# K^T V products as four 64x64 tiles, K rectified in place, and routing split into single steps, in a fused attention and adapter kernel

## The chip, the cores and the metric

The kernel runs on one core of a Trainium2 chip. A core has TensorE for matrix products (PE in the profile; its weight loads stand apart as PEld), VectorE (DVE), ScalarE (ACT), GpSimd (POOL, which here issues the loads from memory) and SyncE (SP, which issues the stores). The metric is the time of one execution on the device, in microseconds, as the median of several runs. The profile is of one execution and counts from its first instruction to its last; that span is a little shorter than the time.

## The reference

Two parts, one after the other. First a linear attention over 8 batches, 8 heads, 576 positions and 64 values per head; q and k are rectified and weighted with a cosine and a sine of the position. Then a layer that picks 2 of 8 small adapters for each of the 4608 rows and adds their output.

```python
def phi(x, c, s):
    r = np.maximum(x, 0.0)
    return np.concatenate([r * c, r * s], axis=-1)
q_p = phi(q, cos_w, sin_w)
k_p = phi(k, cos_w, sin_w)
kv = np.einsum('bhsf,bhsd->bhfd', k_p, v)
z = np.sum(k_p, axis=2)
num = np.einsum('bhsf,bhfd->bhsd', q_p, kv)
den = np.einsum('bhsf,bhf->bhs', q_p, z)[..., None] + 1e-06
x = num / den                       # then laid out as 4608 x 512
# ... (cut: the layer that picks adapters)
logits = x @ w_gate                 # 8 logits a row, the best 2 are kept
# w = softmax over the kept two
delta = sum over kept e of w[e] * ((x @ A[e]) @ B[e])
out = x + delta
```

The cosine and the sine are put on V instead of K, so that K needs the rectifier alone: each V row becomes `V*cos, cos` and `V*sin, sin` (2 x 65 columns), and K^T times that gives kv and z at once.

## The kernel before

Every piece of work is a step of a plan: an engine, an emitter, what it needs and which buffers it uses. Three tables, found ahead of time and written into the file, fix everything that a scheduler would choose: ORDER is the order of all steps (and so of the instructions on each engine, which run in that order), CHOICE takes one of the engines that a step may run on, and SLOTS gives each use its buffer. HOLD lists (store, load): the store waits until that load has landed.

The loads cast from 32 to 16 bits on their way. For a batch b: K is rectified into a second buffer KR whose order is position block, head, value; V is scaled twice into VV; two steps `kv`, one for each pair of heads a, multiply; and each of these is copied out of PSUM by two steps `kvev` into BD, a block-diagonal operand for the products with q.

```python
POOLS = {"V": 4, "K": 3, "KR": 3, "Q": 5, "VV": 3, "BD": 4, ..., "OSB": 6, ..., "pND": 2, "pS": 4}

def relu_k(eng, hs, uk, ukr):                       # K -> KR
    i = tK[S_(uk)][:, hs[0]:hs[-1] + 1]
    o = tKR[S_(ukr)].rearrange("p j c d -> p c j d")[:, hs[0]:hs[-1] + 1]
    # ACT: activation Relu;  DVE: max with 0

def kv_mm(a, ukr, uvv, up):                         # 18 matmuls, 64 rows x 128 columns, 260 wide
    for j in range(J):                              # J = 9
        for par in range(2):
            r = slice(64 * par, 64 * par + 64)
            nc.tensor.matmul(
                out=pt[:, par, 0:4 * W], lhsT=kt[r, j, 2 * a:2 * a + 2, :],   # W = 65; two heads side by side
                rhs=vt[r, 2 * a:2 * a + 2, j, :][:, :, :, 0:W],               # (views shortened here)
                start=(j == 0), stop=(j == J - 1), skip_group_check=True)

def kv_evac(a, hh, up, ubd, eng):                   # 64 x 260, one head
    o = tBD[S_(ubd)][r, :, a, :, 66 * hh:66 * hh + W]
    i = pND[S_(up)][r, :, hh * 2 * W:(hh + 1) * 2 * W]
```

A matmul there multiplies two heads with two heads (128 x 260), and half of that product, head times the other head's V, is never read.

The rest works on 36 groups of 128 rows. A group goes through: transposes of q (`qt`), rectifier while copied out (`qtev`, ACT), times the tangent (`tan`, DVE), products with BD (`num`), reciprocal of den (`rden`, DVE), `xt` = num times that (DVE), transposes (`xT`), copy (`xTev`), logits and A products of up to three groups (`za`), routing, `zgT`, and the sum with B products (`dx`), copied out (`osb`) and stored. The last nine groups take half of their rows from batch 6 and half from batch 7, so they need kv of both. The routing of three groups:

```python
def r_max(uza, n, um):
    for i in range(n):
        nc.vector.max(out=m8[:, i], in_=lg[:, i])                 # best logits of each row
    nc.vector.tensor_reduce(out=tNA..., in_=m8[:, 0:n, 0:2], ...)  # minus the sum of the two best
    nc.vector.scalar_tensor_tensor(out=tTT..., in0=lg, scalar=2.0, in1=tNA..., ...)
def r_zg(uza, n, uw, uzg):
    nc.vector.tensor_tensor(out=w, in0=mask_v(uza, n), in1=tSG..., op=ALU.mult)
    nc.vector.tensor_tensor(out=tZG..., in0=za_v(...), in1=w..., op=ALU.mult)
# between the two: a sigmoid on ACT, and a mask on DVE
```

`r_max` is one step of the plan and so is `r_zg`: their instructions stand directly behind each other, and each reads what the one ahead of it wrote.

Of the kernel before, what the change touches and what calls it, by code (L numbers as in the profile page):

```python
# [11 lines left out]
BF16 = mybir.dt.bfloat16  # L12
# [8 lines left out]
    17, 32, 14, 15, 1, 19, 27, 16, 20, 0, 34, 2, 18, 26, 9, 11, 13, 23, 10, 45, 35, 3, 4, 33, 31, 30, 22, 12, 28, 7,  # L21
    24, 21, 29, 50, 8, 46, 5, 48, 49, 44, 51, 37, 52, 36, 38, 6, 62, 25, 41, 39, 40, 63, 142, 43, 134, 143, 150, 42,
    64, 158, 135, 144, 151, 145, 136, 159, 53, 86, 137, 146, 152, 160, 138, 139, 75, 147, 153, 140, 154, 148, 155, 47,
    76, 161, 149, 156, 141, 157, 162, 56, 163, 74, 55, 164, 57, 422, 58, 165, 87, 54, 182, 174, 423, 183, 166, 59,
    167, 425, 184, 175, 168, 190, 60, 61, 198, 191, 176, 169, 88, 65, 192, 177, 170, 171, 178, 179, 193, 172, 194,
    199, 185, 173, 180, 67, 98, 181, 424, 437, 66, 186, 187, 214, 99, 230, 200, 215, 71, 426, 231, 216, 427, 232, 188,
    72, 206, 195, 428, 189, 433, 438, 100, 207, 201, 89, 434, 429, 439, 440, 202, 73, 431, 208, 430, 203, 68, 432,
    441, 196, 79, 110, 70, 442, 204, 69, 222, 443, 209, 205, 78, 444, 223, 448, 445, 217, 210, 449, 224, 446, 111,
    218, 211, 197, 262, 254, 263, 451, 219, 454, 255, 264, 212, 447, 220, 256, 225, 455, 221, 453, 238, 213, 226, 112,
    227, 270, 233, 239, 77, 435, 228, 456, 271, 246, 457, 240, 83, 247, 458, 229, 248, 470, 85, 272, 84, 234, 235,  # L30
    459, 80, 450, 460, 471, 123, 91, 472, 236, 81, 463, 82, 465, 237, 473, 241, 474, 464, 461, 466, 242, 243, 475,
    249, 462, 469, 90, 244, 476, 257, 468, 245, 122, 477, 250, 251, 286, 479, 478, 258, 259, 481, 287, 278, 480, 265,
    452, 279, 482, 252, 260, 253, 92, 266, 280, 261, 288, 267, 485, 124, 93, 101, 94, 268, 273, 486, 269, 95, 488,
    274, 487, 275, 489, 276, 96, 294, 302, 97, 277, 490, 295, 289, 102, 491, 281, 303, 492, 290, 296, 496, 282, 493,
    103, 494, 497, 502, 495, 318, 283, 326, 319, 310, 291, 104, 311, 320, 327, 503, 107, 106, 328, 105, 304, 504, 113,
    334, 109, 284, 292, 108, 505, 305, 506, 285, 297, 293, 306, 312, 507, 335, 342, 298, 299, 508, 343, 114, 300, 313,
    115, 513, 301, 511, 307, 518, 314, 315, 321, 519, 509, 329, 322, 323, 514, 336, 119, 344, 510, 330, 331, 520, 512,
    308, 521, 316, 522, 121, 337, 515, 120, 317, 126, 523, 345, 524, 324, 309, 332, 338, 339, 525, 325, 529, 333, 346,
    347, 527, 526, 125, 533, 484, 530, 127, 528, 116, 531, 340, 534, 532, 118, 348, 128, 117, 536, 349, 535, 341, 537,
    131, 130, 129, 538, 350, 133, 374, 539, 351, 358, 132, 540, 359, 352, 544, 375, 360, 398, 353, 541, 545, 399, 361,  # L40
    376, 546, 354, 355, 366, 382, 362, 367, 542, 363, 390, 383, 400, 356, 377, 391, 500, 368, 384, 543, 369, 498, 378,
    392, 357, 406, 370, 414, 371, 407, 364, 550, 436, 379, 365, 415, 385, 408, 551, 372, 393, 553, 373, 386, 387, 483,
    380, 552, 566, 554, 381, 409, 394, 499, 395, 555, 388, 501, 567, 556, 396, 401, 517, 569, 397, 410, 416, 548, 559,
    568, 402, 389, 570, 557, 516, 560, 580, 403, 467, 558, 571, 411, 547, 561, 572, 404, 581, 564, 575, 405, 549, 583,
    562, 417, 582, 576, 563, 584, 412, 577, 413, 565, 573, 418, 419, 578, 585, 594, 574, 586, 420, 595, 587, 579, 421,
    589, 597, 596, 588, 591, 598, 610, 590, 592, 599, 611, 600, 605, 593, 601, 613, 612, 602, 606, 614, 617, 604, 603,
    615, 607, 608, 616, 618, 609, 620, 619, 621,
]
CHOICE = [
    0, 0, 0, 0, 0, 0, 0, 0, 0, 0, 0, 0, 0, 0, 0, 0, 0, 0, 0, 0, 0, 0, 0, 0, 0, 0, 0, 0, 0, 0, 0, 1, 0, 0, 0, 1, 0, 0,  # L50
    0, 1, 0, 0, 1, 1, 0, 0, 0, 1, 0, 1, 0, 0, 0, 0, 0, 0, 0, 0, 1, 0, 1, 0, 0, 0, 0, 1, 0, 0, 0, 0, 0, 0, 0, 0, 0, 0,
    0, 0, 0, 0, 0, 0, 0, 0, 0, 0, 0, 0, 0, 0, 0, 0, 0, 0, 0, 0, 0, 0, 0, 0, 0, 0, 0, 0, 0, 0, 0, 0, 0, 0, 0, 0, 0, 0,
    0, 1, 0, 0, 0, 0, 0, 0, 0, 0, 0, 0, 0, 0, 0, 1, 0, 0, 1, 1, 0, 0, 0, 0, 0, 0, 0, 1, 0, 0, 0, 0, 0, 0, 0, 1, 0, 0,
# [3 lines left out]
    0, 0, 0, 0, 0, 0, 0, 0, 0, 0, 0, 1, 0, 0, 0, 0, 0, 0, 0, 0, 0, 0, 0, 0, 0, 0, 0, 0, 0, 0, 0, 0, 0, 0, 0, 1, 0, 0,  # L57
    0, 0, 0, 0, 0, 0, 0, 0, 0, 0, 0, 0, 0, 0, 0, 0, 0, 0, 0, 0, 0, 0, 0, 0, 0, 0, 0, 0, 0, 0, 0, 0, 0, 0, 0, 0, 0, 1,
    0, 0, 0, 0, 0, 0, 0, 1, 0, 0, 0, 0, 0, 0, 0, 0, 0, 0, 0, 0, 0, 0, 0, 0, 0, 0, 0, 0, 0, 0, 0, 0, 0, 0, 0, 0, 0, 0,
    0, 0, 0, 0, 0, 0, 0, 0, 0, 0, 0, 0, 0, 0, 0, 0, 0, 0, 0, 0, 0, 0, 0, 0, 0, 0, 0, 0, 0, 0, 0, 0, 0, 0, 0, 0, 0, 0,  # L60
    0, 0, 0, 0, 0, 0, 0, 0, 0, 0, 0, 0, 0, 0, 0, 0, 0, 0, 0, 0, 0, 0, 0, 0, 0, 0, 0, 0, 0, 0, 0, 0, 0, 0, 0, 0, 0, 0,
    0, 0, 0, 0, 0, 0, 0, 0, 0, 0, 0, 0, 0, 0, 0, 0, 0, 0, 0, 0, 0, 0, 0, 0, 1, 0, 1, 0, 0, 0, 0, 0, 0, 0, 0, 0, 0, 0,
    0, 0, 0, 0, 0, 0, 0, 0, 0, 0, 0, 0, 0, 0, 0, 0, 0, 0, 0, 0, 0, 0, 0, 0, 0, 0, 0, 0, 0, 0, 0, 0, 0, 0, 0, 0, 0, 0,
    0, 0, 0, 0, 0, 0, 0, 1, 0, 1, 0, 0, 0, 0, 0, 0, 0, 0, 0, 0, 0, 0, 0, 0, 0, 0, 0, 0, 0, 0, 1, 0, 0, 0, 0, 0, 0, 0,
    0, 0, 0, 0, 0, 0, 0, 0, 0, 0, 0, 0, 0, 0, 0, 0, 1, 0, 0, 0, 1, 0, 0, 0, 0, 0, 0, 0, 0, 0, 0, 0, 0, 1, 1, 0, 0, 0,
    0, 0, 0, 0, 0, 0, 0, 0, 0, 0, 0, 0, 0, 0,
]
SLOTS = [
    3, 1, 0, 2, 0, 0, 0, 0, 0, 0, 0, 1, 1, 1, 1, 1, 1, 1, 1, 0, 2, 2, 2, 2, 2, 0, 2, 0, 1, 3, 3, 1, 0, 1, 3, 1, 0, 0,
    4, 0, 1, 0, 0, 0, 2, 1, 0, 2, 2, 0, 1, 1, 0, 2, 1, 1, 0, 1, 2, 0, 1, 3, 2, 0, 1, 0, 3, 1, 1, 1, 1, 1, 0, 0, 0, 0,  # L70
    0, 0, 0, 1, 1, 1, 2, 2, 1, 2, 2, 2, 2, 3, 3, 0, 1, 3, 3, 3, 3, 6, 1, 0, 4, 2, 4, 2, 5, 0, 2, 5, 0, 5, 0, 4, 0, 0,
    6, 1, 0, 0, 7, 1, 1, 7, 2, 1, 3, 0, 1, 2, 8, 0, 2, 0, 3, 1, 0, 9, 1, 3, 2, 1, 0, 1, 10, 0, 4, 3, 6, 1, 2, 11, 1,
    5, 0, 2, 0, 0, 12, 2, 0, 3, 4, 0, 1, 13, 0, 1, 3, 3, 1, 2, 14, 2, 2, 0, 7, 0, 0, 15, 1, 3, 1, 5, 1, 1, 2, 0, 4, 0,
    0, 1, 2, 0, 2, 5, 3, 6, 0, 1, 1, 3, 0, 2, 1, 1, 0, 3, 1, 1, 1, 2, 1, 1, 5, 1, 2, 0, 4, 0, 2, 4, 2, 3, 3, 5, 1, 0,
    7, 1, 4, 2, 3, 0, 1, 8, 0, 5, 1, 7, 1, 2, 6, 1, 0, 2, 0, 1, 0, 9, 3, 1, 0, 1, 0, 1, 10, 2, 2, 2, 6, 0, 2, 11, 3,
    3, 1, 2, 1, 0, 12, 0, 4, 3, 3, 1, 2, 14, 2, 5, 3, 4, 0, 1, 13, 0, 0, 2, 7, 1, 0, 0, 0, 1, 1, 0, 0, 2, 2, 3, 2, 1,
    5, 0, 0, 15, 3, 3, 2, 1, 1, 1, 1, 3, 4, 1, 6, 0, 2, 5, 2, 5, 1, 0, 0, 0, 2, 0, 1, 0, 0, 2, 3, 1, 1, 1, 1, 1, 1, 1,
    3, 0, 2, 0, 0, 0, 3, 0, 2, 2, 1, 3, 0, 1, 1, 1, 1, 1, 3, 3, 1, 0, 3, 0, 0, 0, 3, 0, 2, 4, 3, 1, 0, 1, 1, 1, 3, 1,
    1, 5, 3, 2, 0, 0, 0, 0, 3, 0, 3, 1, 0, 2, 1, 1, 1, 1, 0, 1, 0, 1, 0, 2, 3, 0, 0, 0, 2, 0, 3, 0, 2, 2, 1, 1, 1, 1,
    1, 1, 1, 3, 1, 2, 0, 0, 0, 0, 0, 0, 0, 4, 1, 2, 3, 1, 1, 1, 3, 1, 2, 5, 1, 0, 0, 0, 0, 0, 0, 3, 2,  # L80
# [3 lines left out]
    (435, 74), (451, 76), (452, 88), (484, 122), (500, 124),  # L84
# [65 lines left out]
def kernel(  # L150
# [10 lines left out]
    nc = tc.nc  # L161
# [20 lines left out]
    def sb(shape, dtype, name, n=None):  # L182
        if n is None:
# [4 lines left out]
    POOLS = {"V": 4, "K": 3, "KR": 3, "Q": 5, "VV": 3, "BD": 4, "QT": 8, "XT": 16, "XTT": 6,  # L188
             "ZG": 2, "ZGT": 2, "OSB": 6, "M8": 2, "W": 2, "RD": 3,
# [24 lines left out]
    tKR = sb([128, J, 4, D], BF16, "KR", POOLS["KR"])  # L214
# [16 lines left out]
    def S_(u):  # L231
        return pl.slot[u]
# [125 lines left out]
    pl.add("w", [("DVE", 0.6, w_aw("DVE")), ("ACT", 0.8, w_aw("ACT"))], 3, needs=["Ald", "Gld"], makes=["AW"])  # L358
# [25 lines left out]
    def relu_k(eng, hs, uk, ukr):  # L384
        def f():
            i = tK[S_(uk)][:, hs[0]:hs[-1] + 1]
            o = tKR[S_(ukr)].rearrange("p j c d -> p c j d")[:, hs[0]:hs[-1] + 1]
            if eng == "ACT":
                nc.scalar.activation(o, i, AF.Relu)
            else:  # L390
                nc.vector.tensor_scalar(out=o, in0=i, scalar1=0.0, scalar2=None, op0=ALU.max)
        return f

    def vscale(eng, cs, hs, uv, uvv):
        def f():
# [6 lines left out]
            else:  # L402
                nc.vector.tensor_tensor(out=o, in0=i, in1=TV[:, cs].unsqueeze(1).to_broadcast([128, n, J, D]), op=ALU.mult)  # L403
        return f

    def kv_mm(a, ukr, uvv, up):
        def f():
            kt, vt, pt = tKR[S_(ukr)], tVV[S_(uvv)], pND[S_(up)]
            for j in range(J):
# [328 lines left out]
```

## Time and profile before

The time is 117.64 us, the median of 3 runs (116.33 to 118.29). The profiled execution has a span of 115.4 us.

| Engine | busy us | share of the span | instructions |
|---|---|---|---|
| PE, matmuls | 96.9 | 84% | 1383 |
| PEld, weight loads | 68.8 | 60% | 1394 |
| DVE | 95.6 | 83% | 273 |
| ACT | 83.0 | 72% | 182 |
| POOL | 25.7 | 22% | 41 |

The page also has the span cut into 40 equal slices of 2.9 us, in which a digit is a tenth of busy time, and the chain of work that ended last, followed back from the end. Matmuls overlap in the array, so the busy time of PE is not what it could do at best; it is read together with when the matmuls start. In the lines of groups, the two numbers behind the first bar are the busy time of the group in us and the mean duration of one instruction in ns, and behind the second bar stands the idle time of the engine just ahead of them.

### The profile page before, as it was taken

What the parts mean: (1) busy time and instruction counts of PE and PEld (TensorE: products, weight loads), DVE (VectorE), ACT (ScalarE), POOL (GpSimd) and SP (SyncE); (2) the same over time, 40 slices, a digit from 0 to 9 for tenths busy, and PEclk for the clock granted to TensorE, in tenths of its full rate; (3) what the DMA queues carried; (4) which work ended last, traced back from release to release, by engine and by line L of the source; (5) the groups of instructions that cost most, each with busy time, mean ns of one, the idle gap of its engine ahead of it and who ended that gap; (6) DMA issues with size and microseconds to landing.
All of it is one profiled execution on the core that took longest, in us unless ns stands there. A gap on an engine that the chain in (4) does not pass through costs nothing.

```text
span 115.4 us, 3462 instructions
## 1 busy us (share of the span) xinstructions
PE 96.9 (84%) x1383; PEld 68.8 (60%) x1394; DVE 95.6 (83%) x273; ACT 83.0 (72%) x182; POOL 25.7 (22%) x41
## 2 busy tenths in 40 slices
PE   0999957679669999999999998979999999998600
PEld 0344445567556577876587787757676788665100
DVE  6823479979799999999999999999998999998700
ACT  5639477266947899979676889997846975989400
POOL 5997766352022222222200000000000000000000
PEclk9999999999999999999999999999999999999995
DMA  0999999999999999999999999999384298989991
GB/s 3 146 134 193 192 204 206 207 208 207 209 206 208 207 209 206 227 302 242 213 303 230 208 208 207 211 204 256 115 185 87 54 226 264 288 247 240 419 411 51
DMA packets 17039, 24.08 MB, mean 209 GB/s; under 512 B 2176, under 2 KB 14592, under 8 KB 17024
## 3 DMA queue, kind: packets, MB, share of 16 engines
q0 software_dynamic: 14096, 14.43, 75.7%
q1 hardware_dynamic: 2928, 9.44, 26.1%
q8 instruction: 11, 0.18, 0.6%
q14 instruction: 4, 0.03, 0.1%
HBM read 28.85 MB, written 9.44 MB: 332 GB/s over the span
## 4 chain that ended last, share of the span: by engine, by line
PE 43%; DVE 21%; DMA 14%; ACT 9%; issue 5%; POOL 3%; POOLq 0%; ACTq 0%; DVEq 0%
DMA Kb<-in_k_dram 14%; PE pnd L506 10%; PE pnd L412 10%; PE ps L530 5%; PE ps L476 5%; PE ps L602 4%; DVE xt L522 4%; DVE VV L403 4%; PE ps L543 4%; DVE qTcs L493 3%; PE ps L604 3%; ACT qTcs L481 3%; PE ps L591 2%; DVE zg L582 2%; ACT osb L242 2%
## 5 line engine op out<-in xcount | busy, mean ns | idle before, releaser
L522 DVE TENSOR_TENSOR xt<-pnd,rden 128x512 bf16<-128x512 f32 x36 | 24.3, 687 | 0.8
L506 PE MATMUL pnd<-BD,qTcs 128*128 128x130 bf16 (+1 forms) x384 | 22.5, 223 | 2.9 <-DVE xt L522 2.4
L481 ACT ACTIVATE qTcs<-ps 128x512 bf16<-128x512 bf16 x36 | 20.3, 602 | 5.5 <-PE ps L476 5.3
L403 DVE TENSOR_TENSOR VV<-Vb,TV 128x2304 bf16<-128x2304 bf16 (+1 forms) x17 | 19.1, 1135 | 4.0 <-DMA Vb<-in_v_dram 4.0
L506 PEld LDWEIGHTS <-qTcs 128*128 128x128 bf16 (+1 forms) x384 | 18.0, 103 | 6.2 <-issue 3.7
L412 PE MATMUL pnd<-VV,KR 64*128 64x260 bf16 x288 | 19.3, 272 | 2.7 <-DVE VV L403 1.2
L242 ACT COPY xT<-ps 128x512 bf16<-128x512 bf16 x30 | 17.1, 587 | 2.3 <-PE ps L530 1.9
L242 ACT COPY osb<-ps 128x512 f32<-128x512 f32 (+1 forms) x31 | 16.4, 574 | 1.9 <-DVE osb L244 0.9
L412 PEld LDWEIGHTS <-KR 64*128 64x128 bf16 x288 | 13.3, 93 | 6.8 <-issue 2.5
L493 DVE TENSOR_TENSOR qTcs<-qTcs,TT 128x512 bf16<-128x512 bf16 x36 | 14.0, 409 | 1.3 <-ACT qTcs L481 0.7
L530 PE MATMUL ps<-ident,xt 128*128 128x128 bf16 x144 | 13.3, 223 | 0.7 <-DVE xt L522 0.6
L602 PE MATMUL ps<-xt,ident 128*128 128x512 bf16 x35 | 13.1, 380 | 0.7 <-DVE osb L244 0.3
L424 ACT CAST BD<-pnd 64x260 bf16<-64x260 f32 x24 | 9.0, 376 | 5.6 <-PE pnd L412 4.5
L476 PE MATMUL ps<-ident,Qb 128*64 128x128 bf16 x288 | 11.9, 222 | 1.0 <-DMA Qb<-in_q_dram 0.7
L297 PE MATMUL ps<-warm 128*128 128x512 bf16 x34 | 9.2, 435 | 3.1 <-DVE warm L291 3.1
L401 ACT ACTIVATE VV<-Vb,TVf 128x128 bf16<-128x128 bf16 (+1 forms) x27 | 9.2, 433 | 3.5 <-DMA Vb<-in_v_dram 3.5
L530 PEld LDWEIGHTS <-xt 128*128 128x128 bf16 x144 | 9.5, 116 | 3.6 <-DVE xt L522 1.5
L476 PEld LDWEIGHTS <-Qb 128*64 128x64 bf16 x288 | 8.8, 109 | 4.5 <-issue 2.8
L543 PE MATMUL ps<-AW,xT 128*128 128x136 bf16 x144 | 10.8, 223 | 0.3 <-ACT xT L242 0.2
L543 PEld LDWEIGHTS <-xT 128*128 128x128 bf16 x144 | 9.1, 98 | 2.3 <-issue 0.8
L604 PE MATMUL ps<-Ball,zgT 128*128 128x512 bf16 x26 | 9.7, 379 | 0.4 <-ACT zgT L242 0.4
L297 PEld LDWEIGHTS <-warm 128*128 128x128 bf16 x34 | 3.6, 109 | 7.9 <-DVE warm L291 3.1
(54 smaller groups left out, 107.2 us busy)
## 6 DMA issues: line engine op xcount, KB each, us to landing
out_dram<-osb SPq DMA_DIRECT2D x16, 256.0 KB, 4.5
Kb<-in_k_dram POOLq DMA_DIRECT2D x6, 576.0 KB, 22.8
Vb<-in_v_dram POOLq DMA_DIRECT2D x6, 576.0 KB, 24.8
Qb<-in_q_dram POOLq DMA_DIRECT2D x6, 576.0 KB, 24.8
out_dram<-osb SPq DMA_DIRECT2D x6, 384.0 KB, 4.5
out_dram<-osb SPq DMA_DIRECT2D x2, 768.0 KB, 5.7
Kb<-in_k_dram POOLq DMA_DIRECT2D x4, 288.0 KB, 7.4
Vb<-in_v_dram POOLq DMA_DIRECT2D x4, 288.0 KB, 6.9
```

What stands on the lines that cost most here:

```text
L242: nc.scalar.copy(o, i)
L403: nc.vector.tensor_tensor(out=o, in0=i, in1=TV[:, cs].unsqueeze(1).to_broadcast([128, n, J, D]), op=ALU.mult)
L412: nc.tensor.matmul(out=pt[:, par, 0:4 * W], lhsT=kt[r, j, 2 * a:2 * a + 2, :].rearrange("p h d -> p (h d)"), rhs=vt[r, 2 * a:2 * a + 2, j, ...
L476: nc.tensor.transpose(out=pt[64 * hh:64 * hh + 64, a, :, x], in_=qt[:, c, j, :], identity=ident)
L481: nc.scalar.activation(tQT[S_(uqt)][:, 0].rearrange("p i x s -> p (i x s)"), pB(up)[:, 0:512], AF.Relu)
L493: nc.vector.tensor_tensor(out=v[1], in0=v[0], in1=f4, op=ALU.mult)
L506: nc.tensor.matmul(out=nd[r, a, 0:4 * W].rearrange("p (h e w) -> p h e w", h=2, e=2)[:, :, par], lhsT=s[:, r], rhs=bd[:, par, a, cs].rearr ...
L522: nc.vector.tensor_tensor(out=tXT[S_(uxt)].rearrange("p (a h d) -> p a h d", a=2, h=4), in0=nd_view(und)[:, :, :, 0:D], in1=tRD[S_(urd)].u ...
L530: nc.tensor.transpose(out=pB(up)[:, c * 128:(c + 1) * 128], in_=tXT[S_(uxt)].rearrange("p (x c) -> p c x", c=4)[:, c], identity=ident)
L543: nc.tensor.matmul(out=pF(uza)[:, n * AW_W:(n + 1) * AW_W], lhsT=tXTT[S_(u)][:, c, :], rhs=AW[:, c, :], start=(c == 0), stop=(c == 3))
L602: nc.tensor.matmul(out=pF(udx), lhsT=ident, rhs=tXT[S_(uxt)], start=True, stop=False)
L604: nc.tensor.matmul(out=pF(udx), lhsT=tZGT[S_(uzt)][:, i], rhs=Ball, start=False, stop=True)
```

## The change

Three things, and a new plan found with them.

The product of K and V is taken for each head alone: 64 rows of K by its 64 values, times the 130 columns of its own V. Row half `par` and head `hh` choose one of the four 64x64 quarters of the array, and four matmuls that follow each other go to four different quarters. Nothing unread is computed. One PSUM buffer holds all four heads that share a row half, so that a batch needs one buffer and two copies of twice the size.

K is rectified where it lies. The buffers KR are gone; K has four buffers, OSB seven.

The routing is split into the steps `max`, `sum`, `diff`, `mask`, `w`, `zg`, so that the plan may put other work between an instruction and the one that reads its result; the plan counts the time that such a result takes on the same engine.

```diff
-    (435, 74), (451, 76), (452, 88), (484, 122), (500, 124),      # HOLD
+    (454, 87), (512, 105),                                        # the loads of Q 5 and of Q 7
...
-    POOLS = {"V": 4, "K": 3, "KR": 3, "Q": 5, ... "OSB": 6, ...
+    POOLS = {"V": 4, "K": 4, "Q": 5, ... "OSB": 7, ...
...
-            i = tK[S_(uk)][:, hs[0]:hs[-1] + 1]
-            o = tKR[S_(ukr)].rearrange("p j c d -> p c j d")[:, hs[0]:hs[-1] + 1]
+            k_ = tK[S_(uk)][:, hs[0]:hs[-1] + 1].rearrange("p c j d -> p (c j d)")
...
-    def kv_mm(a, ukr, uvv, up):
+    def kv_mm(aa, uk, uvv, up):
+            for a in aa:
+                for j in range(J):
+                    for par in range(2):
+                        for hh in range(2):
+                            r = slice(64 * par, 64 * par + 64)
+                            nc.tensor.matmul(
+                                out=pt[64 * hh:64 * hh + 64, par, a * 2 * W:(a + 1) * 2 * W], lhsT=kt[r, 2 * a + hh, j, :],
+                                rhs=vt[r, 2 * a + hh, j, :].rearrange("p (c w) -> p c w", c=2)[:, :, 0:W],
+                                start=(j == 0), stop=(j == J - 1), skip_group_check=True)
...
-    def kv_evac(a, hh, up, ubd, eng):
+    def kv_evac(hh, up, ubd, eng):
-            i = pND[S_(up)][r, :, hh * 2 * W:(hh + 1) * 2 * W].rearrange("p e (c w) -> p e c w", c=2)
+            i = pND[S_(up)][r, :, 0:4 * W].rearrange("p e (x w) -> p e x w", w=W)
...
+    def r_sum(n, um):        # the tensor_reduce of r_max
+    def r_diff(uza, n, um):  # its scalar_tensor_tensor
+    def r_w(uza, n, uw):     # the first instruction of r_zg
```

The rest of the diff is the three tables ORDER, CHOICE and SLOTS (all of their numbers differ) and the lines that enter the new steps into the plan. Batches 0 and 1 are still loaded and multiplied in two halves, the others in one piece.

## The prediction

> **What bounds the kernel now.** I read the slices first, then the chain of waits, then the groups, and for DVE the timeline.
>
> ```profile
> PE   0999957679669999999999998979999999998600
> ...
> DVE  6823479979799999999999999999998999998700
> ACT  5639477266947899979676889997846975989400
> ...
> DMA  0999999999999999999999999999384298989991
> GB/s 3 146 134 193 192 204 206 207 208 207 209 206 208 207 209 206 227 302 242 213 303 230 208 208 207 211 204 256 115 185 87 54 226 264 288 247 240 419 411 51
> ```
>
> Up to slice 10 (about 30 us) the engines have gaps and DMA has none: the kernel lives on what arrives. From there to 105 us PE and DVE are both full. DMA stays full to slice 27, which ends at 81 us: that is the input. Its last load (Q of batch 7) is issued at 57.0 us, and loads of its kind take 24.3 us to land (the view of that line): 81.3.
>
> ```profile
> PE 43%; DVE 21%; DMA 14%; ACT 9%; issue 5%; POOL 3%; POOLq 0%; ACTq 0%; DVEq 0%
> DMA Kb<-in_k_dram 14%; PE pnd L506 10%; PE pnd L412 10%; PE ps L530 5%; PE ps L476 5%; PE ps L602 4%; DVE xt L522 4%; DVE VV L403 4%; PE ps L543 4%; DVE qTcs L493 3%; PE ps L604 3%; ACT qTcs L481 3%; PE ps L591 2%; DVE zg L582 2%; ACT osb L242 2%
> ```
>
> The K^T V products (L412) are 10% of the chain, 11.2 us. The chain in order of time shows them in its late part:
>
> ```profile
> 67.31 2.13 PE pnd L412 x36
> 69.44 0.34 PE ps L476 x8
> ...
> 82.89 1.12 PE pnd L412 x18
> 84.01 0.57 PE ps L530 x8
> 84.58 2.13 PE pnd L412 x36
> ```
>
> So 18 of them take 1.07 to 1.12 us, 59 to 62 ns each. DVE's timeline shows how it pays for a result of its own:
>
> ```profile
> 46.24 0.16 DVE L559 TENSOR_REDUCE nasum<-m 128x3 f32<-128x6 f32 x1
> 46.44 0.18 DVE L561 SCALAR_TENSOR_TENSOR tt<-ps,nasum 128x24 f32<-128x24 f32 x1
> 46.54 0.20 DVE L517 RECIPROCAL rden<-pnd 128x8 f32<-128x8 f32 x1
> 46.77 0.69 DVE L522 TENSOR_TENSOR xt<-pnd,rden 128x512 bf16<-128x512 f32 x1
> 47.38 0.75 DVE L391 TENSOR_SCALAR KR<-Kb 128x2304 bf16<-128x2304 bf16 x1
> ...
> 82.20 0.75 DVE L391 TENSOR_SCALAR KR<-Kb 128x2304 bf16<-128x2304 bf16 x1
> 90.00 0.69 DVE L522 TENSOR_TENSOR xt<-pnd,rden 128x512 bf16<-128x512 f32 x1
> ```
>
> L517 needs nothing of L561 and starts 0.08 us before that ends (46.54 against 46.62). L522 reads what L517 writes and starts 0.03 us after it ends. A result read at once costs 0.11 us.
>
> The last two rows give the end its shape. K of batch 7 lands one load (0.59 MB at 207 GB/s, 2.85 us) ahead of Q 7, at 78.5, but DVE rectifies it only at 82.2: the engines are 3.7 us behind the input. The first of the last nine groups gets its xt at 90.0, the last copy begins at 109.5, and the last store ends the span at 115.4.
>
> **What the skill says.** In "TensorE: Matmul & The Clock Gate", Part 3 (packing small matmuls), matmuls on different tiles of the array overlap and a pack lasts one matmul plus some 4 ns for each further tile. The trace agrees for two tiles: the two row halves of L412 start 4 ns apart, a pair every 111 ns (260 columns), and the transposes of q (L476, two column halves, 128 columns) give a pair every 56 ns. Four tiles are in no run yet. "TensorEngine Tiling (Array Packing)", Key Properties, has a change of tiling mode drain the array; here the step between L476 and L412 is about 0.1 us longer than within a group. "VectorE: DVE Perf Modes", "The DRAIN you can't avoid", says that a same-engine read of a fresh result needs a semaphore or an instruction between; the 0.11 us above is its price here. The overview page, "Trainium Kernel Development and Optimization", Key Constraints, has all queues share 16 DMA engines; the slices show stores at 46 to 63 us beside slower loads.
>
> **The change part by part.**
>
> *PE.* Before: 16 steps of 18 matmuls, 16 x 1.08 = 17.3 us. After: 576 matmuls of 130 columns, four at a time. From the 56 ns of a 128-column pair, four take 57 + 2 x 4, some 62 ns; 18 fours a batch make 1.1 us, with start and end 1.2; 8 x 1.2 = 9.6. Six to eight fewer entries into the mode save another 1. PE: -8.5 us, of which the 11.2 us of chain lose about half, 5.5.
>
> *DVE.* Counts come from the order of instructions of both kernels, durations from the groups. Two fewer full rectifiers (807 ns): -1.6. Copies to BD: 8 of 422 ns become 4 twice as wide, at an estimated 690: -0.6. One more full V product and one half fewer (1342, 756): +0.6. One 512-wide and one 256-wide osb fewer (681, 421): -1.1. A small copy more: +0.2. Together -2.5. Then the results read at once: rden-xt 24 before, 11 after; max-sum 13 to 4; sum-diff 13 to 1; w-zg 13 to 3; one new: 63 to 20, 43 x 0.11 = -4.7. DVE: -7.2 us.
>
> *ACT.* BD: 24 of 376 become 12 at about 590, -1.9; two more full rectifiers at 2116, +4.2; V parts -0.9; osb +1.0. ACT: +2.4 on 83, with room (72%).
>
> *Input.* The order of loads changes: at the start both halves of K, V for batches 0 and 1 come before the adapters' weights and the second half of Q 1, so batch 1 may be multiplied a little earlier, perhaps 1 us of the early gaps of DVE. At the end it is K 7, V 7, Q 7 instead of V 7, K 7, Q 7. And with two holds instead of five, more is stored before V 7: 2.43 MB instead of 1.66 by the order and the sizes of the stores. In slices 16 to 21, the 1.66 MB lifted the rate by 275 GB/s x 2.9 us = 0.8 MB above the loads' 207, so they pushed the loads back by 0.87 MB, 4.2 us, 2.5 us a MB. 0.77 MB more: 1.9 us. V 7 then lands at about 80.4.
>
> *The path to the end.* From V 7: two V products on DVE 2.6, kv 1.2, copies 0.65, num 0.6, rden 0.2, and some 0.4 between engines: 5.7, with other work in between 6.4. First xt of the last nine at 86.8 instead of 90.0. By DVE alone (7.2 us less, a good third of it later than this point) it would be about the same, 86 to 87: the backlog of 3.7 us is used up here, and the rest of what DVE and PE win cannot come before the input. After that point before needs 19.5 us to the last copy. The new order has moved ahead of it one routing, one `za` (0.71), four transposes of q (4 x 0.27), one `dx` (0.44), one `zgT`: 2.4 us less for PE, and for DVE about 2.2 and a further 1 of results read at once. I take 2.2: 17.3. Last copy at 104.1, and 5.9 from there to the end as before: span 110.0. The engines alone would give 115.4 - 7.2 = 108.2. I lean to the input path but give the other a third: 109.4. Time is 2.2 above the span (117.64, 115.4): 111.6.
>
> **The rivals.**
>
> *Four tiles do not run together.* If heads that share a row half take turns, a four lasts 2 x 57 = 114 ns, a batch 2.1 us, and PE gets nothing. For it: two heads load weights into the same rows, and no four is in the trace. Against: the two column halves of L476 share all rows and still pair fully. PE stays full; time about 115.5.
>
> *The input holds everything.* Loads end at the same time or later whatever the engines do. For it: DMA is full for 78 us. Against: 34 us of work follow the last landing, and part of them is backlog. If more stores delay the loads by 4 us instead of 1.9, the time is about 113.5.
>
> *ACT becomes the wait.* The new rectifiers of 2.1 us stand in line before copies of q that PE and DVE wait for ("ACT qTcs L481" 3% of the chain already). Each may cost its neighbours a microsecond: about 114.
>
> *The plan is simply better packed, input and all:* 109.
>
> **Range and chances.** Both engines that are full lose 7 to 8 us, and only the input keeps part of it back, so the direction is well founded; the size hangs on the landing of V 7 and on how well the new order fits real durations. Predicted 111.6 us, range 108.8 to 115.2. Faster by over 2% (under 115.3) 0.89, within 2% 0.09, slower by over 2% 0.02.
>
> **What would show it.** Right: 72 K^T V matmuls of a batch in 1.1 to 1.3 us; DVE busy about 93 (only the 2.5 counts as busy time, the rest is gaps and overlap), a chain with far less L412, DMA full to 81 to 84 us, the first xt of the last nine at 86 to 88, and some 17 us to the last copy. Wrong: 2 us a batch; or new idle of PE behind ACT's rectifier; or a first xt later than 89.

## The result and the profile after

The changed kernel takes 113.45 us (median of 4 runs, 113.06 to 115.27) beside 117.35 us of the kernel before: ratio 0.968, 95% interval 0.959 to 0.978. A second set gave 113.08 us and 0.965 (0.959 to 0.971). Predicted were 111.6 us and a range of 108.8 to 115.2: the direction and the range held, the gain is 3.9 us instead of 5.7 to 6.0.

The slices of the profiled execution, span 111.5 us:

```profile
PE   2998953679974999999799999889998799999820
...
DVE  6806228975799999979999998999899999998730
ACT  5182997958994699998559939996996798747820
...
PEclk9999999976999999999999999999999999999995
DMA  0999999999999999999999999999969894789892
```

The picture is the old one: DMA full to slice 28 (counted from 0), which ends at 80.8 us as slice 27 did before, PE and DVE full from 30 us on. New are lower digits of DVE at the start and a clock of 0.7 and 0.6 in two slices; in the trace the granted clock is 0.50 from 23.8 to 27.2 us. The chain of waits, by engine and by line:

```profile
PE 41%; DVE 21%; ACT 20%; DMA 7%; issue 6%; POOL 2%; ACTq 0%; POOLq 0%
PE pnd L507 10%; DMA Vb<-in_v_dram 7%; ACT qTcs L482 6%; PE ps L531 6%; PE pnd L413 6%; PE ps L613 5%; DVE xt L523 5%; ACT VV L400 5%; PE ps L544 5%; DVE VV L402 5%; PE ps L615 4%; PE ps L477 3%; ACT xT L242 3%; DVE qTcs L494 2%; DVE BD L427 2%
```

The K^T V products (now L413) fell from 10% to 6%, and ACT rose from 9% to 20%. The chain in order of time shows what they cost now, and the end of batch 7:

```profile
65.00 1.17 PE pnd L413 x71
...
86.77 0.72 DVE BD L427
87.51 0.60 ACT BD L425
88.16 1.10 PE pnd L507 x31
```

A whole batch of 72 products (71 of them are on the chain) takes 1.17 us, where 36 of the old ones took 2.13. The two copies out of PSUM follow each other, although they are on two engines: ACT waits for DVE's. DVE's timeline:

```profile
75.95 0.18 DVE L518 RECIPROCAL rden<-pnd 128x8 f32<-128x8 f32 x1
76.06 0.16 DVE L563 TENSOR_REDUCE nasum<-m 128x3 f32<-128x6 f32 x1
76.17 0.69 DVE L523 TENSOR_TENSOR xt<-pnd,rden 128x512 bf16<-128x512 f32 x1
...
79.47 0.70 DVE L390 TENSOR_SCALAR Kb<-Kb 128x2304 bf16<-128x2304 bf16 x1
...
82.12 1.35 DVE L402 TENSOR_TENSOR VV<-Vb,TV 128x2304 bf16<-128x2304 bf16 x1
83.39 0.68 DVE L244 COPY osb<-ps 128x512 f32<-128x512 f32 x1
83.99 1.35 DVE L402 TENSOR_TENSOR VV<-Vb,TV 128x2304 bf16<-128x2304 bf16 x1
...
89.71 1.28 DVE L523 TENSOR_TENSOR xt<-pnd,rden 128x512 bf16<-128x512 f32 x2
```

In the first three rows the sum of the routing stands between a reciprocal and the xt that reads it, and each starts 0.05 to 0.07 us ahead of the end of the one before: the 0.11 us are gone. K of batch 7 is rectified at 79.5 instead of 82.2. But the first xt of the last nine groups comes at 89.7, hardly ahead of the 90.0 of before.

That splits the time into four: up to the fifth xt, from there to the first of the last nine groups, from there to the last copy, and the wait for the last store. Busy time of each engine in the first three, the kernel before first (columns: from and to, length, PE, PEld, DVE, ACT, POOL with their instructions, clock, DMA share, GB/s):

```profile
0.00:30.06 30.06, 22.99 (x258) 14.28 (x259) 20.04 (x55) 18.65 (x41) 19.05 (x32) 1.00 1.10 172
30.06:90.00 59.94, 55.88 (x860) 41.96 (x869) 57.74 (x154) 48.89 (x108) 6.66 (x9) 1.00 1.09 209
90.00:109.88 19.88, 17.99 (x273) 12.58 (x270) 17.77 (x66) 15.42 (x35) 0.00 (x0) 1.00 0.86 257
```

The kernel after:

```profile
0.00:30.38 30.38, 23.15 (x330) 14.81 (x330) 17.82 (x43) 21.83 (x51) 18.97 (x32) 0.94 1.09 171
30.38:89.71 59.33, 53.67 (x1118) 41.24 (x1123) 57.53 (x168) 48.55 (x95) 6.66 (x9) 1.00 1.14 227
89.71:107.85 18.14, 16.33 (x237) 10.76 (x234) 15.43 (x57) 13.11 (x29) 0.00 (x0) 1.00 0.82 263
```

| | start | middle | last nine groups | last store | span |
|---|---|---|---|---|---|
| before, us | 30.1 | 59.9 | 19.9 | 5.6 | 115.4 |
| after, us | 30.4 | 59.3 | 18.1 | 3.7 | 111.5 |

DVE loses 4.8 us of busy time in all (95.55 to 90.79): 2.2 in the first 30 us, 0.2 in the middle, 2.3 at the end. The start gets no shorter by its 2.2, DVE idles there instead. A V product of half a batch and two copies of xT went to ACT there (its busy time rises from 18.65 to 21.83), and one routing's max, sum, difference and mask, some 0.9 us, are left to the middle. The middle, where DVE is 97% busy, also takes a routing and a product with the tangent of the last nine groups and a V product from ACT, and gives ACT two rectifiers. From the counts of instructions and their mean durations I estimate that 2.2 us of DVE work came in on balance, about as much as the stretch saved: it gets 0.6 us shorter.

### The profile page after: what moved, and what is told of

Same layout as the page of the kernel before. It is cut to its first block, busy times and chain, and to the rows that moved or that the text cites. A ratio compares the mean times of both kernels' runs of the same rounds, so it can differ in the third digit from the quotient of the medians.

```text
span 111.5 us, 4005 instructions
## 1 busy us (share of the span) xinstructions
PE 93.1 (84%) x1674; PEld 66.8 (60%) x1682; DVE 90.8 (81%) x266; ACT 83.5 (75%) x173; POOL 25.6 (23%) x41
## 4 chain that ended last, share of the span: by engine, by line
PE 41%; DVE 21%; ACT 20%; DMA 7%; issue 6%; POOL 2%; ACTq 0%; POOLq 0%
PE pnd L507 10%; DMA Vb<-in_v_dram 7%; ACT qTcs L482 6%; PE ps L531 6%; PE pnd L413 6%; PE ps L613 5%; DVE xt L523 5%; ACT VV L400 5%; PE ps L544 5%; DVE VV L402 5%; PE ps L615 4%; PE ps L477 3%; ACT xT L242 3%; DVE qTcs L494 2%; DVE BD L427 2%
## 5 line engine op out<-in xcount | busy, mean ns | idle before, releaser
L507 PE MATMUL pnd<-BD,qTcs 128*128 128x130 bf16 (+1 forms) x384 | 23.3, 225 | 3.6 <-ACT BD L425 2.4
L242 ACT COPY osb<-ps 128x512 f32<-128x512 f32 (+1 forms) x33 | 17.6, 577 | 1.8 <-DVE osb L244 1.1
L413 PE MATMUL pnd<-VV,Kb 64*64 64x130 bf16 x576 | 10.5, 222 | 2.7 <-DVE xt L523 1.5
L531 PEld LDWEIGHTS <-xt 128*128 128x128 bf16 x144 | 10.4, 117 | 3.7 <-DVE xt L523 0.9
L425 ACT CAST BD<-pnd 64x520 bf16<-64x520 f32 x12 | 7.2, 597 | 6.4 <-PE pnd L413 3.4
L413 PEld LDWEIGHTS <-Kb 64*64 64x64 bf16 x576 | 9.3, 108 | 4.2 <-issue 2.2
L297 PE MATMUL ps<-warm 128*128 128x512 bf16 x34 | 10.0, 461 | 2.0 <-DVE warm L291 2.0
L615 PE MATMUL ps<-Ball,zgT 128*128 128x512 bf16 x29 | 11.0, 379 | 0.4 <-DVE zgT L244 0.3
L388 ACT ACTIVATE Kb<-Kb 128x2304 bf16<-128x2304 bf16 (+1 forms) x5 | 8.8, 1760 | 2.0 <-DMA Kb<-in_k_dram 2.0
L400 ACT ACTIVATE VV<-Vb,TVf 128x128 bf16<-128x128 bf16 x27 | 8.2, 389 | 2.5 <-DMA Vb<-in_v_dram 2.5
```

The source lines that it names most:

```text
L242: nc.scalar.copy(o, i)
L413: nc.tensor.matmul(out=pt[64 * hh:64 * hh + 64, par, a * 2 * W:(a + 1) * 2 * W], lhsT=kt[r, 2 * a + hh, j, :], rhs=vt[r, 2 * a + hh, j, :] ...
L507: nc.tensor.matmul(out=nd[r, a, 0:4 * W].rearrange("p (h e w) -> p h e w", h=2, e=2)[:, :, par], lhsT=s[:, r], rhs=bd[:, par, a, cs].rearr ...
L531: nc.tensor.transpose(out=pB(up)[:, c * 128:(c + 1) * 128], in_=tXT[S_(uxt)].rearrange("p (x c) -> p c x", c=4)[:, c], identity=ident)
L615: nc.tensor.matmul(out=pF(udx), lhsT=tZGT[S_(uzt)][:, i], rhs=Ball, start=False, stop=True)
```

## The experiments

The ratios are to the kernel before, in runs beside it on the same chip; the twelve ran in three sets of four, in the order in which they stand here. The profile of each is of one execution. Medians are of all executions; ratios leave out those more than 1.5% above the fastest of their kernel, so where I give a difference in us it is worked out from the ratios.

**The changed kernel again**, to compare with. No edit.

> The changed kernel once more, beside the others of this set, so that they can be compared with it on one chip. Every theory: 0.968 of the kernel before, 113 to 114 us; first product-with-V copies and the first xt at the same places as in the profile already seen.

Measured: 113.08 us, 0.965 (0.959 to 0.971); start 29.8, middle 59.4, last nine groups 18.1, last store 3.7. As expected.

**Two tiles instead of four.**

```diff
-                for j in range(J):
-                    for par in range(2):
-                        for hh in range(2):
+                for hh in range(2):
+                    for j in range(J):
+                        for par in range(2):
```

> The changed kernel with the head loop outside, so that only two of the 64x64 matmuls (the two row halves) can run side by side; same instructions, same order of everything else. A batch should then take about 36 x 57 = 2.05 us instead of 1.2, the cost of the kernel before. Theory A (VectorE sets the pace from 30 us on, the matrix engine has room): 0 to 1.5 us slower, because only waits of single batches, the last one above all (0.9), are on the path. Theory B (the matrix engine sets the pace): 8 x 0.9 = 7 us slower, all of the gain gone.

Measured: 115.95 us, 0.9875 (0.981 to 0.994), so 2.6 us slower than with four: between both theories. PE's timeline of this kernel, and then of the changed one:

```profile
47.78 1.69 PE L413 MATMUL pnd<-VV,Kb 64*64 64x130 bf16 x72
```

```profile
46.15 1.24 PE L413 MATMUL pnd<-VV,Kb 64*64 64x130 bf16 x72
```

A batch takes 0.45 us more, not 0.85: eight of them make 3.6 us, and the kernel pays 2.6. The middle stretch takes it (63.3 us, of which a stretch of lower clock has about 1.7, see *The new order alone*):

```profile
30.10:93.40 63.30, 57.54 (x1119) 45.20 (x1124) 57.77 (x168) 48.64 (x95) 6.67 (x9) 0.97 1.07 215
```

DVE is as busy as with four tiles (57.77, 57.53) and now idles 5.5 of 63.3 us, the lower clock's part included. So PE has little room to spare: 2.6 us is more than theory A allows.

**The routing in one piece.** Sum and difference again directly behind max, the weight directly ahead of zg; the other steps emit nothing and the order stays.

```diff
     def r_max(uza, n, um):
+            nc.vector.tensor_reduce(out=tNA[S_(um)][:, 0:n], ...)            # from r_sum
+            nc.vector.scalar_tensor_tensor(out=tTT[S_(um)][:, 0:n], ...)     # from r_diff
     def r_zg(uza, n, uw, uzg):
+            nc.vector.tensor_tensor(out=tW[S_(uw)][:, 0:n], ...)             # from r_w
```

> The changed kernel with the routing put together again: sum and difference directly behind max, weight directly ahead of zg; nothing else moves. 36 more VectorE instructions read the result of the one just ahead, at 0.11 us each: 4.0 us more on VectorE. Theory A (VectorE sets the pace): 2.5 to 4 us slower, which undoes the whole gain. Theory C (the input sets the pace and VectorE only looks full): under 1 us slower.

Measured: 115.31 us, 0.979 (0.971 to 0.987): 1.6 us slower, two fifths of the 4.0 us put on DVE, less than theory A has and more than theory C. Its middle:

```profile
29.80:92.20 62.40, 55.01 (x1118) 42.18 (x1123) 59.68 (x168) 48.82 (x95) 6.78 (x9) 0.97 1.09 218
```

DVE has 2.15 us more to do there than in the changed kernel and the stretch is 3.1 us longer, about 1.0 of it by a stretch of lower clock. The other 2.1 us are about what DVE got to do, so it has no room: theory C is out for this stretch.

**The kernel before with the tiles alone.**

```diff
-                    nc.tensor.matmul(out=pt[:, par, 0:4 * W], lhsT=kt[r, j, 2 * a:2 * a + 2, :] ..., rhs=vt[r, 2 * a:2 * a + 2, j, :] ...)
+                    for hh in range(2):
+                        nc.tensor.matmul(out=pt[64 * hh:64 * hh + 64, par, 0:2 * W], lhsT=kt[r, j, 2 * a + hh, :], rhs=vt[r, 2 * a + hh, j, :] ...)
...
-            i = pND[S_(up)][r, :, hh * 2 * W:(hh + 1) * 2 * W]
+            i = pND[S_(up)][r, :, 0:2 * W]
```

> The kernel before with only its K^T V products taken as 64x64 tiles of one head each, four at a time (same order, same buffers, same copies of half the used width out of PSUM). The 18.6 us of its 16 products shrink to about 9.6. Theory A: 0 to 1.5 us faster. Theory B: 4 to 7 us faster, as the 10% share of these products in its chain of waits suggests.

Measured: 114.46 us, 0.975 (0.969 to 0.981): 2.9 us faster, between the theories again, and seven tenths of what the whole change brings. Start 29.3, middle 59.1, last nine 19.9, last store 3.9. Its middle:

```profile
29.30:88.40 59.10, 51.76 (x1072) 39.21 (x1081) 57.17 (x153) 48.60 (x108) 6.93 (x9) 1.00 1.12 216
```

PE has 4.1 us less to do than before (55.88), and the stretch is only 0.8 shorter; DVE fills 97% of it. The start gave 0.8 and the wait for the last store 1.7. The first xt of the last nine is at 88.4, earlier than in the changed kernel (89.7), which makes up for it after that point.

**Less input late.** K and V of batches 4 to 7 and Q of 5 to 7 are loaded in part (5 of 9 position blocks).

```diff
+                if b >= (5 if u[0] == "Q" else 4):
+                    return nc.gpsimd.dma_start(out=flat(ts[S_(u)])[:, :, 0:5 * D], in_=full_src(x, b)[:, :, 0:5 * D])
```

> The changed kernel with less input late: K and V of batches 4 to 7 and Q of batches 5 to 7 are loaded for 5 of the 9 position blocks only, the rest stays what an earlier batch left there (part of the input is left out). 11 loads of 2.85 us shrink by 4/9, so the last ones land about 14 us earlier. Theory C (the engines follow the input up to batch 7): 3 us or more faster. Theory D (engines that wait for each other set the pace, the input is 1.5 to 2 us ahead of them at batches 5 to 7): at most 1 us faster, from stores that meet fewer loads.

Measured: 113.64 us, 0.961 (0.952 to 0.970): the time of the changed kernel. Its DMA in the slices, and its middle:

```profile
DMA  0999999999999999999999999000009975798993
```

```profile
30.60:90.00 59.40, 54.18 (x1124) 41.28 (x1123) 57.62 (x168) 48.62 (x95) 6.68 (x9) 1.00 0.92 176
```

DMA is full for four slices (11 us) less. V 7 lands at 66.0 instead of 81.0 (issued at 51.3 and 55.0, 14.7 and 26.0 us to landing), and the first xt of the last nine groups is at 90.0 all the same. The landing of V 7, on which the prediction built its path to the end, holds nothing up.

**Another start.** K and V of batch 0 first, two V products from ACT to DVE, and the steps that this frees moved up.

```diff
-    17, 42, 19, 14, 20, 1, 16, 32, 0, 15, 2, 33, 28, 27, 45, 3, 34, ...    # ORDER: K 1, K 0, V 0, Q 0, V 0, Q 0 ...
+    17, 32, 19, 14, 20, 1, 16, 26, 0, 15, 2, 33, 27, 28, 3, 34, ...        # ORDER: K 0, K 0, V 0, V 0, Q 0, Q 0 ...
+    # CHOICE[30] = CHOICE[53] = 0; steps 29, 38, 41, 40, 45 and 53 moved
```

> The changed kernel with another start: both halves of K and V of batch 0 first, then Q 0, K of batch 1 behind; one V product each of batches 0 and 1 goes from ScalarE (2.6 us) to VectorE (0.66), and the rectifier of the second K half, the products and their copies move up. The first xt should come at about 17 instead of 20 us, and the idle time of VectorE up to 30 us (12.5 us, against 10.0 in the kernel before) should fall below 10.5. Theory D: 1 to 2 us faster, up to where V 5 and V 7 bind. Theory C: under 0.5 us faster.

Measured: 0.966 (0.956 to 0.977), no gain. Batch 0 was ready earlier, but I had put V products of batch 1 ahead of its first reciprocal, as DVE's timeline shows:

```profile
18.81 1.43 DVE L401 TENSOR_TENSOR VV<-Vb,TV 128x1152 bf16<-128x1152 bf16 x2 [1.38 <-DMA Vb<-in_v_dram]
20.27 0.21 DVE L517 RECIPROCAL rden<-pnd 128x8 f32<-128x8 f32 x1
20.51 0.69 DVE L522 TENSOR_TENSOR xt<-pnd,rden 128x512 bf16<-128x512 f32 x1
```

DVE stood 1.38 us for a load while the group behind it could have run, and the fifth xt is at 30.9, no earlier than without. The test failed to make the start that it was meant to test.

**The clock kept up.**

```diff
+    def fill(pt, n):
+        for _ in range(n):
+            nc.tensor.matmul(out=pt[:, 0, 260:512], lhsT=warm[:, 0:128], rhs=warm[:, 0:252], start=True, stop=True, ...)
+            fill(pt, {(0, 0): 8, (1, 1): 10}.get((uk[1], aa[0]), 0))                          # in kv_mm
+            fill(nd, {("one", 0, 0): 14, ("one", 0, 2): 6, ("one", 0, 3): 4}.get(g, 0))       # in num_mm
```

> The changed kernel with 42 products of ones added where the matrix engine waits between 14 and 26 us (they write PSUM columns that nothing reads), so that its granted clock should stay full in the slices at 22 to 28 us, where it fell to 0.6 to 0.7. If the dip costs what it looks like (72 products in 1.6 instead of 1.24, two groups of transposes at half speed, VectorE waiting 1.15 us for a product): 1 us faster. If the dip is in the shadow of the input: the same within 0.5.

Measured: 0.971 (0.960 to 0.981), no gain. The granted clock in its slices:

```profile
PEclk9999999999999999999999999999999999999999
```

The dip is gone and nothing is won: the fifth xt comes at 31.2, where it came at 30.4 and 29.8 in the two profiles of the changed kernel, so the added products cost more than they won. From there to the first xt of the last nine it is 59.6 us, as ever.

**Two copies off the end.** CHOICE of steps 529 and 543 (osb of two groups) from DVE to ACT.

```diff
+    # CHOICE[529] = CHOICE[543] = 0
```

> The changed kernel with two of VectorE's copies to osb, which stand directly ahead of and between the two V products of batch 7, given to ScalarE at the same places. The first xt of the last nine groups should come 1.2 us earlier (from 89.7), if V 7 at 81.0 allows it: the V products could begin at 81.5 instead of 82.1. Theory D: 0.6 to 1.2 us faster. If ScalarE is the one that these groups wait for: the same or slower.

Measured: 0.960 (0.951 to 0.969), within the interval of the changed kernel. The profile shows why nothing is won. From the last pair of xt ahead of the last nine groups to the first of these, in this kernel and then in the changed one:

```profile
82.07:91.44 9.37, 8.57 (x198) 6.20 (x197) 8.17 (x21) 8.36 (x19) 0.00 (x0) 1.00 0.62 164
```

```profile
80.32:89.71 9.39, 8.28 (x198) 6.18 (x197) 9.08 (x23) 7.57 (x17) 0.00 (x0) 1.00 0.84 203
```

DVE has 0.9 us less to do and ACT 0.8 more, and the length is the same. Just ahead of the last nine groups DVE is not what they wait for. The chain there runs over PE, in this kernel also over the copies of ACT:

```profile
82.81 1.96 ACT osb L241 x4
```

**The start planned again.** As in *Another start*, but with the four groups of batch 0 ahead of the V products of batch 1, the weights loaded before batch 1, and the routing of the first three groups moved up; three uses get other PSUM buffers.

```diff
+    # ORDER: 17, 32, 19, 14, 20, 1, 16, 26, 0, 15, 2, 33, 27, 28, 34, 3, ..., 22, 42, 23, 49, ...   (K 0, K 0, V 0, V 0, Q 0, Q 0, A, K 1, gate, V 1 ...)
+    # CHOICE[30] = CHOICE[53] = 0
```

> The changed kernel with its start planned again by hand: both halves of K, V and Q of batch 0, then the adapters' weights, then batch 1; all V products but one on VectorE; the four groups of batch 0 ahead of the V products of batch 1, and the routing of the first three groups behind them, where VectorE stood idle. Theory E (from the fifth xt on the engines run at a pace of their own, 59.3 us to the first of the last nine groups, and what the first 30 us leave undone is paid later): first xt at 17 to 18 instead of 20 us, VectorE idle up to 30 us under 10.5 instead of 12.5 us, 1.5 to 2.5 us faster than the changed kernel. If the first 30 us are bound by what has landed: the same within 0.5.

Measured: 114.35 us, 0.975 (0.969 to 0.980), 1% slower than the changed kernel. DVE's timeline:

```profile
19.04 0.69 DVE L523 TENSOR_TENSOR xt<-pnd,rden 128x512 bf16<-128x512 f32 x1
...
24.84 0.32 DVE L558 MAX8 m<-ps 128x8 f32<-128x8 f32 x3 [0.92 <-PE ps L544]
25.07 0.74 DVE L402 TENSOR_TENSOR VV<-Vb,TV 128x1152 bf16<-128x1152 bf16 x1
...
27.84 0.70 DVE L427 CAST BD<-pnd 64x520 bf16<-64x520 f32 x1 [0.97 <-PE pnd L413]
```

The first xt is 0.7 to 1.2 us earlier than in the two profiles of the changed kernel, but the routing waits 0.92 us for its logits with two V products of batch 1 behind it. So the products of batch 1 come late, and the fifth xt is at 32.5 instead of 30.4; DVE idles 12.0 us before 30 us, about as much as ever. Whether the start can be filled at all stays open: neither order of mine did it.

**The new order alone.** Both savings taken back at once: the edits of the second and the third experiment together.

```diff
+    # heads outside (two tiles), and sum, difference and weight in one piece
```

> The changed kernel with both of its savings taken back, as in the two earlier runs (two tiles side by side instead of four; routing in one piece): what stays is the new order of loads, steps and stores, K rectified in place, and the copies of double width. If the parts add up: 113.1 + 2.9 + 2.2 = 118.2, about 1 us slower than the kernel before. If the two savings overlap (each hides behind the other): 116 to 117.

Measured: 116.54 us, 0.990 (0.986 to 0.993). Start 29.9, middle 62.7, last nine 18.3, last store 3.3. Its middle:

```profile
29.90:92.60 62.70, 57.15 (x1123) 43.81 (x1122) 59.67 (x167) 48.53 (x95) 6.67 (x9) 1.00 1.09 217
```

The two savings seem to need each other: with neither the middle takes 62.7 us, with one of them 62.4 or 63.3, with both 59.3. But the clock differs. The kernels with one saving have a stretch of half clock in the middle, the two others have none. The row of it for the two tiles:

```profile
35.90:39.30 3.40, 3.35 (x74) 2.89 (x74) 3.22 (x10) 0.77 (x2) 0.74 (x1) 0.51 1.21 208
```

Two neighbouring xt on both sides of it, with two tiles and then here, where the clock is full:

```profile
37.12 0.67 DVE L523 TENSOR_TENSOR xt<-pnd,rden 128x512 bf16<-128x512 f32 x1
42.15 0.68 DVE L523 TENSOR_TENSOR xt<-pnd,rden 128x512 bf16<-128x512 f32 x1
```

```profile
37.42 0.68 DVE L523 TENSOR_TENSOR xt<-pnd,rden 128x512 bf16<-128x512 f32 x1
40.73 0.68 DVE L523 TENSOR_TENSOR xt<-pnd,rden 128x512 bf16<-128x512 f32 x1
```

They lie 5.03 us apart there and 3.31 here; 4.30 with the routing in one piece, 3.37 in the changed kernel. So I put 1.7 and 1.0 us down to the lower clock. Without it, I estimate the middle at 61.6 us with the split alone and 61.4 with the tiles alone. Each saving alone then brings some 1.1 and 1.3 us, and both 3.4: 1.0 us more than their sum, by single executions. In times, the split alone brings the new order 0.2% (0.990 to 0.9875), the tiles alone 1.1% (to 0.979), both 2.5% (to 0.965); this gap of 1.2% is about two standard errors, and part of it is the clock, whose mean was 0.984 or more in every execution counted for this kernel and 0.956 to 0.970 in three of the seven counted for the kernels with one saving. So it is not shown that the two help each other. What is left with neither (the order, K in place, copies of double width) is 1% faster than the kernel before.

**The old order with tiles and a split by hand.**

```diff
+            LATER.append(({uza, um}, lambda: nc.vector.tensor_reduce(...)))            # also the difference, and zg's product
...
+            if s.eng == "DVE" and waiting:
+                LATER.pop(0)[1]()           # one of them behind the next step of VectorE, sooner if its buffer is needed
```

> The kernel before, its order kept, with 64x64 tiles and with the sum, the difference and the product behind the routing's weight each moved one or two VectorE instructions back (34 fewer results read at once, 3.7 us). Theory E: the tiles alone gave 3.0; the split gives another 1.5 to 2.2, as it cost 2.2 to take it out of the changed kernel: 112.3 to 113, as fast as the changed kernel or faster, with the start of the kernel before. If the order is what makes the split worth something: no more than 0.5 beyond the tiles, 114 to 114.5.

Measured: 119.81 us, 1.017 (1.009 to 1.025): 4.9 us slower than the tiles alone, though by the traces 42 fewer results are read at once (22, 64). How long PE sat idle for zg before its transposes, in this kernel, and then in the one with the tiles alone (us in total, times):

```profile
  DVE zg L585: 14.7, 17
```

```profile
  DVE zg L583: 5.6, 11
```

The 39 instructions that were to move back (sum, difference and zg of 13 routings) start 15.8 us in all after what they read has ended, with the tiles alone 1.4. Three stand behind a V product of 1.3 us, the others behind something shorter, or behind one that waits itself; and ACT's sigmoid, PE's transposes and all that follows wait with them. Some 0.1 us each was won, and up to 1.6 given for it. Both expectations were wrong.

**The old order without holds.**

```diff
-HOLD = [(435, 74), (451, 76), (452, 88), (484, 122), (500, 124)]
+HOLD = []
```

> The kernel before without its five holds: stores go out when their rows are ready. Loads then share with more stores and land later, but a run with the late input 14 us earlier was no faster, so the input has slack; and the stores left for the end get fewer. Theory E: the time from the last copy to the end falls from 5.6 to about 4 us and the kernel is 0.5 to 1.7 us faster. If the holds protect something that counts: slower, and the first xt of the last nine later than 90.

Measured: 117.35 us, 1.001 (0.998 to 1.005), no difference. The wait for the last store was 4.7 instead of 5.6 us in its profile, the first xt of the last nine at 89.7. In the old order the holds neither help nor hurt, and fewer of them is not what the change gains by.

## Why the prediction was right or wrong

*The tiles* were right to the decimal: a batch of 72 in 1.24 us where 1.2 was predicted, four starting every 58 ns where 62 was reckoned (its sum, 57 + 2 x 4, is 65). The rival that they do not run together is out. The group of K^T V matmuls fell from 19.3 to 10.5 us of busy time, but PE as a whole only from 96.9 to 93.1.

*The results read at once*: with those of the routing back, the middle is 2.1 us longer (the lower clock's part left out), about what DVE got to do there. But the term "DVE: -7.2 us" was read as time. DVE's busy time fell 4.8 us (90.8 measured, "about 93" predicted), and its idle time before the last copy rose by 2.7 (14.3 to 17.1): net 2.0. ACT gained 0.5 us, not 2.4.

*The input, "perhaps 1 us of the early gaps of DVE"*, had the wrong sign: DVE is busy 2.2 us less in the first 30 us, which are no shorter. Of the profile of before I had used the early gaps as a reserve, and not asked what the new order puts into them.

*The path to the end* is the step that failed: "First xt of the last nine at 86.8 instead of 90.0" was 89.7. Its ground was the landing of V 7. Predicted at 80.4 it came at 81.0, but its first product on DVE began only at 82.1, and from there it was 7.6 us to the xt instead of 6.4; and with V 7 at 66.0 the xt is no earlier. So the landing is not what that xt waits for. The other estimate, "by DVE alone" 86 to 87 (7.2 less a good third of it makes it 85 to 86), failed too: ahead of that xt DVE has 2.4 us less to do (77.8 to 75.4), 2.2 of it in the first 30 us, where it only made idle time.

What sets the xt is the start and then the middle stretch, where PE at 90 to 93% and DVE at 97% hand work to each other in a fixed order. The middle takes 59.3 to 59.6 us in the five profiles with both savings and the same start, while the fifth xt came anywhere from 29.8 to 32.1 us: what the start loses is not made up. Inside the middle the change saves on both engines, and work moves in, from the start, from the last nine groups and from ACT. That both engines limit the stretch was shown by taking each saving back. That the work moved in is what used up the rest is read from busy times and counts of instructions and not shown: the two experiments on the start, which should have tested it, did not fill it, and the one on the end shows a piece of 9.4 us in which less work for DVE gained nothing.

*After that point* the step was right: 17.8 us to the beginning of the last copy, 17.3 predicted, 19.5 before.

*The last store*: 5.9 was carried over "as before", and the wait from the beginning of the last copy fell to 4.1 us (from its end, as above, from 5.6 to 3.7). This gain of 1.9 us, half of the whole, was not foreseen, and it hides how far off the xt was. Without it I estimate 115.3 us (113.45 + 1.9), at the edge of the range: that the range held is in part luck. The gain is in every variant of the new order (3.1 to 3.7) and also in the old order with tiles (3.9). What is still to be moved when the last copy ends went with it: by the DMA rate of that stretch 1.25 MB before, 0.7 in the new order, 0.8 in the old one with tiles; without the holds it was 0.9 MB, with a wait of 4.7, and no gain. Why less is left over stays open.

*The rivals*: the input as the limit is out. ACT did become more of a wait (20% of the chain instead of 9%), and two copies more for it at the end won nothing, but no run isolates it.

## What to carry to other kernels

When two in-order engines that feed each other are both over 90% busy, a saving on one of them is not simply time. Take each saving out again, one at a time and both at once: here either alone was worth 1.1 to 1.3 us of a stretch of 60, and both 3.4, by estimates from one profile each. Before comparing such runs, look at the granted clock of each stretch: without that, the same runs seemed to show that one saving is worth almost nothing without the other. And look at where a planned order moves work, not only at how much it removes: add up each engine's busy time in stretches that end at the same point of the work, and count the instructions in them, to tell what was saved, what went to another engine and what reappears in the next stretch.

Moving a small dependent instruction away from its source is worth 0.11 us here, and loses more than that as soon as it lands behind a long one while another engine waits for its result.

## What the runs showed of the hardware

With heads outside, 18 products of one head use two tiles, and then the next 18 the other two. A batch should take 36 x 57 ns = 2.05 us; it took 1.69 (the row shown above). In the trace the pairs start every 56 to 62 ns after the first, and around each change of head most of them every 20 to 36 ns: products of the next head run beside those of the last, so the tiles overlap without being interleaved in the program.

What a stretch of half clock cost depended on where it fell. With 3.4 us of it that ended by 24 us the fifth xt came at 29.8 to 30.1 in three profiles, and at 29.9 in one at full clock. With 10.2 us of it there (the kernel with two copies off the end) it came at 32.1. And 3.4 us of it at 36 us, where PE and DVE are both full, went with 1.0 to 1.7 us between two xt, as shown above.
